# One exchange of maxima and sums for q's half rows, another order of the attention's slots, and the weights' sums one tile earlier

## The chip, the cores and the metric

The kernel runs on one core of a Trainium2 chip. The metric is the device time in microseconds (us) of one execution. The kernel before took 883.22 us (median of three runs, 882.94 to 884.86).

## What is computed

Eight batches go through a linear attention with eight heads, 576 rows and head dimension 64, and the 4608 rows that come out go through a feed-forward network with 512 model and 2048 inner columns:

```python
q_s = exp(q - max(q, axis=-1));  q_s = q_s / (sum(q_s, axis=-1) + 1e-09)
k_s = exp(k - max(k, axis=2));   k_s = k_s / (sum(k_s, axis=2) + 1e-09)
kv  = einsum('bhsd,bhse->bhde', k_s, v)
x   = einsum('bhsd,bhde->bhse', q_s, kv)      # rows of 512, one per token
h   = maximum(x @ w_in, 0.0)
out = h * h @ w_out
```

q is normalised along each row of 64 values, k along the 576 tokens. Everything is float32; a matmul is made of three passes over a high and a low part of its operands (wh·xh, wh·xl, wl·xh).

## The kernel before

**Tiles and chunks.** Seven tiles, t = 0 to 6, each take the first 512 tokens of batch t through the feed-forward network. A tile has 16 chunks f of 128 inner columns. In a chunk, TensorE (PE) makes `h` (`first`, line 994, 12 matmuls) and then the 12 matmuls of `second` (line 1016) that add an earlier chunk, f-2, to the four accumulators `acc`. At the beginning of a tile three `first` stand one behind another. ScalarE (ACT) makes `r` (Relu) and `gh` (Square), VectorE (DVE) makes `h` times `r` and `gl` (`split_g`, line 1009). `h` has two banks of PSUM, so `h` of chunk f needs `gl` of chunk f-2 to be done. `end_tile` (line 1328) finishes the last two chunks and stores the accumulators. Behind the seven tiles, the last full batch and a tile of all the remaining tokens are computed together with a Strassen-like scheme of seven products for each pair of chunks (lines 1494 to 1555); its operands (`b11`, `b21`, `t1` to `t4`, `b22`, each with a high and a low part) are prepared by `ahead` (line 1358) in the last chunks of tile 6 and by `late_part` (line 1409) behind it.

**Attention in slots.** Under the feed-forward work of tile t lies the attention of batch t+1, in 16 slots s, one per chunk; slot s belongs to head pair p = s // 4 and step i = s % 4. For batches from 2 on (`prepare`, `step`, `step_between`, `step_after`, lines 1227 to 1300):

- at i = 3 of the pair before: `k_max` on DVE, then `k_shift_pool` (line 737) on GpSimd (POOL): `partition_all_reduce` makes `kmx` from `km`, and k and the tail `kt` are shifted by it. `blocks_max` reduces q's half rows of 32 to their maxima and swaps them with the other half, by four DMAs of SyncE (SP).
- i = 0: `blocks_exp`: the larger maximum, subtraction, exp on ACT, sum, a second exchange of four DMAs.
- i = 1: `blocks_norm` and `blocks_turn` on DVE (transposed into `qT`), `k_exp` on ACT (`ek`), and the loads of the next pair's k and q.
- i = 2: for even p, `blocks_split`: `qh` on ACT and `ql` on POOL; the next pair's v is loaded (a small memset on POOL goes with it). For odd p, `kv_product` (line 880) of both pairs on PE, then `ks`, `kvh`, `kvl`.
- i = 3 of odd p: `x_product` of both pairs on PE.

**Weights' sums.** For the Strassen part, eight sets of sums of `w_in` are made in tiles 2 to 5, two sets a tile (`sums_step`, line 1337): `add_sums` on POOL (`full` and `sums`, six instructions) at f % 8 = 1, the rest at 2 to 4.

**Order.** Outside tile 0, where a planner sorts recorded work, each engine runs its instructions in the order in which the code tells them. Where a helper records a call, all instructions have line 100.

Of the kernel before, what the change touches and what calls it, by code (L numbers as in the profile page):

```python
# [336 lines left out]
def attention_ffn(  # L337
# [290 lines left out]
    def swap_halves(t, name):  # L628

        o = small([P, NG], "sw", f"sw_{name}", 1)  # L630
        for j in range(2):
            for a in range(2):
                at, of = j * D + a * Q, j * D + (1 - a) * Q
                Y.dma_start(out=o[at:at + Q], in_=t[of:of + Q])
        return o

    def blocks_max(b, p):
        mx = small([P, NG], "bmx", f"bmx_{b}_{p}", 1)
        V.tensor_reduce(out=mx, in_=made["q", b, p], op=ALU.max, axis=AX.X)
        made["bmx", b, p] = mx, swap_halves(mx, f"m_{b}_{p}")  # L640

    def blocks_exp(b, p):
        t = made["q", b, p]
        mx, sw = made.pop(("bmx", b, p))
        V.tensor_tensor(out=mx, in0=mx, in1=sw, op=ALU.max)
# [4 lines left out]
        sm = small([P, NG], "bsm", f"bsm_{b}_{p}", 1)  # L650
        V.tensor_reduce(out=sm, in_=t, op=ALU.add, axis=AX.X)
        made["bsm", b, p] = sm, swap_halves(sm, f"s_{b}_{p}")

    def blocks_norm(b, p):
        t = made["q", b, p]
        sm, sw = made.pop(("bsm", b, p))
        V.scalar_tensor_tensor(
            out=sm, in0=sm, scalar=EPS, in1=sw, op0=ALU.add, op1=ALU.add
        )
        V.reciprocal(out=sm, in_=sm)  # L660
        V.tensor_tensor(
            out=t, in0=t, in1=sm.unsqueeze(2).broadcast_to([P, NG, Q]), op=ALU.mult
        )
# [216 lines left out]
    def kv_product(b, p):  # L880
# [14 lines left out]
        with plan.together():  # L895
            for i, (k_part, v_part) in enumerate(parts):
                for j in range(2):
                    rows, cols = slice(j * D, (j + 1) * D), slice(j * D, j * D + n)
                    T.matmul(
                        out=ps[rows, cols], lhsT=k_part[:, rows],  # L900
                        rhs=vr[:, j, i, :] if b == 0 else v_part[:, cols],
                        start=(i == 0), stop=(b > 0 and i == C), n=2 * n,
                    )
            if b == 0:
                for j in range(2):
                    rows = slice(j * D, (j + 1) * D)
                    T.matmul(
                        out=ps[rows, rows], lhsT=ekt[:, rows],
                        rhs=v_heads[tl, 2 * p + j, 0:D].only(p // 2),
                        start=False, stop=True, n=2 * n,  # L910
                    )
        if b == 0:
            ks, at_of = made.pop(("ks", p)), D
        else:
            ks, at_of = small([P, 1], "ks", f"ks_{b}_{p}"), D + 1
            V.tensor_scalar_add(ks, ps[:, D:D + 1], EPS, n=8)
            V.reciprocal(out=ks, in_=ks, n=8)
# [12 lines left out]
        made["kv", b, p] = (kvh, kvl)  # L930

# [203 lines left out]
    def store(t, acc, c):  # L1135
        if c % 2 == 0:
            made["o"] = cvt.tile([P, 2, DM], F32, tag="w", name=f"o_{t}_{c}")
        o = made["o"][:, c % 2, :]
        if t == B and c == C - 1:
            V.tensor_copy(out=o[:, 0:DM // 2], in_=acc[c][:, 0:DM // 2])  # L1140
            S.copy(out=o[:, DM // 2:DM], in_=acc[c][:, DM // 2:DM])
        elif c % 2:
            S.copy(out=o, in_=acc[c])
        else:
            V.tensor_copy(out=o, in_=acc[c])
        if t < B:
            rows = out[t * SQ:t * SQ + M, :].rearrange(
                "(p c) e -> p c e" if t < TB else "(c p) e -> p c e", c=C
            )
            Y.dma_start(out=rows[:, c, :], in_=o)  # L1150
        else:
            per = P // TL
            for j in range(per):
                r0 = (c * per + j) * SQ + M
                queue = S if c == C - 1 and j % 2 else Y
                queue.dma_start(out=out[r0:r0 + TL, :], in_=o[j * TL:(j + 1) * TL, :])
# [40 lines left out]
    for p in range(NP):  # L1197
        plan.ease = p * STEP
        boot_max(p)
        boot_turn(p)  # L1200
        boot_exp(p)
        q_norm(0, p, G)
        kv_product(0, p)
        q_turn(0, p)
        x_product(0, p, x)
# [21 lines left out]
    def prepare(b, p):  # L1227
# [4 lines left out]
        if b >= TB:  # L1232
            blocks_max(b, p)
# [5 lines left out]
    def step(b, s):  # L1239

        p, i = divmod(s, NP)
        if b >= TB:
            if i == 0:
                blocks_exp(b, p)
# [18 lines left out]
    def step_after(b, s, x):  # L1263
# [16 lines left out]
        elif i == 2:  # L1280
            if b >= TB:
                if p % 2:
                    kv_product(b, p - 1)
                    kv_product(b, p)
            else:
                if p == 0:
                    tail_turn(b)
                kv_product(b, p)
# [7 lines left out]
        elif i == 3:  # L1296
            if b < TB or p % 2:
                x_product(b, p, x)
            if p + 1 < NP:
                prepare(b, p + 1)  # L1300
# [36 lines left out]
    def sums_step(t, f, begin=False):  # L1337

        j, i = divmod(f, NF // 2)
        j += 2 * (t - TB)  # L1340
        if t < TB or j >= NF // 2:
            return
        if begin:
            if i == 4:
                rest_sums(j)
            return
        if i == 1:
            add_sums(j)
        elif i == 2:
            begin_sums(j)  # L1350
        elif i == 3:
            split_sums(j)
        elif i == 4:
            keep_sums(j)

    x_of, w_of = {}, {}

    def ahead(f, x):

        k = range(2)  # L1360
        if f == 4:
            for i in range(2):
                to = slabs[X_RAW + i].bitcast(F32)[:, :, 0:(B - 1) * TL]
                Y.dma_start(out=to, in_=x_tail[:, 2 * i:2 * i + 2, 0:(B - 1) * TL])
            w_of[0] = weights(0)
            load_weights(0, w_of[0], "a11", "s1", "a12", "s2")
        elif f == 12:
# [5 lines left out]
            x_of["b11"] = pieces("b11", 0)  # L1373
            split_part(made["b11"], "b11", 0)
            split_part(made["b11"], "b11", 1)
        elif f == 13:
            made["sum"] = [att.tile([P, M], F32, tag=tag, name=f"sum_{tag}") for tag in ("k", "q")]
            for i in k:
                G.tensor_tensor(
                    out=made["sum"][i], in0=made["b12"][i], in1=made["b11"][i], op=ALU.subtract  # L1380
                )
        elif f == 14:
            x_of["t1"] = pieces("t1", 0)
            for i in k:
                split_part(made["sum"], "t1", i)
        elif f == 15:
            load_weights(0, w_of[0], "s3", "a22", "s4")
            for name in ("b21", "t2"):
                x_of[name] = pieces(name, 0)
            split_part(made["b21"], "b21", 0)  # L1390
            G.tensor_tensor(
                out=made["sum"][0], in0=made["b22"][0], in1=made["sum"][0], op=ALU.subtract
            )
            split_part(made["b21"], "b21", 1)
            V.tensor_tensor(
                out=made["sum"][1], in0=made["b22"][1], in1=made["sum"][1], op=ALU.subtract
            )
            for i in k:
                split_part(made["sum"], "t2", i)
            for i in k:  # L1400
                G.tensor_tensor(
                    out=made["b11"][i], in0=made["sum"][i], in1=made["b11"][i], op=ALU.subtract
                )
            for i in k:
                G.tensor_tensor(
                    out=made["b21"][i], in0=made["b21"][i], in1=made["sum"][i], op=ALU.subtract
                )

    def late_part(name, src):

        x_of[name] = pieces(name, 0)
        for i in range(2):
            split_part(made[src], name, i)

    for t in range(WT):
        b = t + 1
        x_next, acc = begin_next(t), begin_acc(t)
        parts = {}
        for f in range(NF):
            h = first(t, f, x)  # L1420
            sums_step(t, f, True)
            if f < LA:
                sums_step(t, f)
# [5 lines left out]
            step(b, f)  # L1429
            plan.due = None  # L1430
            if f >= LA:
                for c in range(C):
                    second(f - LA, parts[f - LA], acc, c)
                    if c == 0:
                        step_between(b, f, x_next)
                sums_step(t, f)
                parts[f] = split_g(t, f, *h)
            plan.due = f + SOON
            step_after(b, f, x_next)
            plan.due = None  # L1440
            if t == WT - 1:
                ahead(f, x_next)
        if t == 0:
            plan.run(SEEDS, fill)
            x = split_x(x_next, b)
        elif t < WT - 1:
            x = split_x(x_next, b)
        if t < WT - 1:
            if b + 1 < B:
                prepare(b + 1, 0)  # L1450
            end_tile(t, parts, acc, NF - 2, NF - 1)
    units = [(t, f, parts[f], acc, c, 0, NF - 1) for f in (NF - 2, NF - 1) for c in range(C)]
# [42 lines left out]
    for n in range(PAIRS):  # L1495
        one, two = 2 * n, 2 * n + 1
        w = w_of.pop(n)
# [6 lines left out]
        if n == 0:  # L1504
            unit(3)
# [3 lines left out]
        if n == 0:  # L1509
            late_part("t3", "b11")  # L1510
        unit(1)
# [6 lines left out]
        unit(1)  # L1518
        product(A, w["s2"], x_of["t2"], False)
        S.copy(out=u2, in_=A)  # L1520
        if n == 0:
            late_part("t4", "b21")
# [4 lines left out]
        unit(1)  # L1527
# [4 lines left out]
        if n == 0:  # L1532
            late_part("b22", "b22")
        else:
            unit(1)
# [77 lines left out]
```

## Time and profile before

| what | value |
|---|---|
| the profiled execution, device time | 882.38 us |
| its span, from the first to the last instruction | 880.2 us |
| median of the runs | 883.22 us |
| mean granted TensorE clock | 0.996 |
| idle DVE before the maxima's exchange, in all | 45.0 us in 18 waits |
| idle DVE before the sums' exchange, in all | 57.2 us in 23 waits |

The profile gives, for each engine, its busy time, and for each idle stretch the instruction or transfer that ended it. An engine that is busy nearly all the time sets the time of the kernel; what the other engines wait for matters only where that engine waits in turn. PE's clock is in the column PEclk, in shares of full speed. In the rows of a timeline the first number is the start in us, the second the duration, and a bracket holds the idle time before the row.

### The profile page before, as it was taken

To read this page: it belongs to the slowest core of one execution; us is meant where nothing else is said; L and a number is where in the kernel's file an instruction comes from. 1 tells how busy PE (TensorE), PEld (TensorE's weight loads), DVE (VectorE), ACT (ScalarE), POOL (GpSimd) and SP (SyncE) were. 2 spreads that over 40 slices of the span, in tenths; PEclk is the share of its full clock that TensorE was granted. 3 is DMA by queue.
4 is the path that set the end of the run, shared out by engine and by line. 5 is a ranking of instruction groups with operands and counts; after the bars stand their busy time and mean duration, and the time that the engine had idled before them with its cause. 6 is when DMAs were issued, how large, how long until landed. Compare 5 with 4: busy or idle time off the path is not lost.

```text
span 880.2 us, 12793 instructions
## 1 busy us (share of the span) xinstructions
PE 858.7 (98%) x4408; PEld 705.6 (80%) x4408; DVE 521.5 (59%) x936; ACT 368.0 (42%) x690; POOL 253.2 (29%) x300
## 2 busy tenths in 40 slices
PE   7899999999999999999999999999999989999997
PEld 7678888888887888788878888888888768888886
DVE  7998976555665566655665566556554783333421
ACT  5888854333434343434433343434333542222221
POOL 6789981111231304140414123130111321010000
PEclk9999999999999999999999999999999999999999
DMA  9991123211241244323331424124341057542432
GB/s 300 381 336 45 33 50 89 43 36 36 79 117 39 74 108 120 86 74 102 107 105 37 114 81 118 40 74 108 83 131 39 6 180 248 168 146 82 156 120 49
DMA packets 168977, 95.54 MB, mean 109 GB/s; under 512 B 117712, under 2 KB 150992, under 8 KB 168912
## 3 DMA queue, kind: packets, MB, share of 16 engines
q1 hardware_dynamic: 167200, 93.41, 36.6%
q10 hardware_dynamic: 1712, 1.31, 0.6%
q8 instruction: 35, 0.57, 0.3%
q14 instruction: 30, 0.25, 0.1%
HBM read 64.88 MB, written 29.23 MB: 107 GB/s over the span
## 4 chain that ended last, share of the span: by engine, by line
PE 72%; DVE 11%; DMA 5%; ACT 4%; SPq 4%; issue 4%; POOL 0%; DVEq 0%; ACTq 0%; POOLq 0%
PE acc L100 34%; PE h L100 24%; PE h L1129 8%; SPq L100 4%; PE x L100 2%; PE kv L100 2%; DMA sw_m<-bmx 2%; DMA sw_s<-bsm 1%; DVE km L100 1%; DVE bsm L100 1%; DVE gl L100 1%; DVE w L100 1%; DVE q L100 1%; DVE bmx L100 1%; ACT q L100 1%
## 5 line engine op out<-in xcount | busy, mean ns | idle before, releaser
L100 PE MATMUL acc<-w,gh 128*128 128x512 f32 x1152 | 355.8, 390 | 0.0
L100 PE MATMUL h<-xh,w 128*128 128x512 f32 x896 | 296.5, 393 | 3.9 <-DVE gl L100 3.8
L100 PEld LDWEIGHTS acc<-w,gh 128*128 128x128 f32 x1152 | 214.9, 188 | 43.8 <-ACT gh L100 0.4
L100 PE MATMUL acc<-w,gl 128*128 128x512 f32 x576 | 224.3, 389 | 0.0
L100 PEld LDWEIGHTS h<-xh,w 128*128 128x128 f32 x896 | 168.2, 188 | 42.7 <-DVE gl L100 7.3
L100 PE MATMUL h<-xl,w 128*128 128x512 f32 x448 | 174.6, 390 | 0.0
L100 PEld LDWEIGHTS acc<-w,gl 128*128 128x128 f32 x576 | 108.1, 188 | 23.1 <-DVE gl L100 0.4
L100 ACT ACTIVATE r<-h 128x512 f32<-128x512 f32 x112 | 66.1, 590 | 78.0 <-PE h L100 77.6
L100 DVE TENSOR_TENSOR gl<-h,gh 128x512 fp32r<-128x512 f32 x112 | 77.0, 688 | 36.4 <-ACT gh L100 29.6
L100 PEld LDWEIGHTS h<-xl,w 128*128 128x128 f32 x448 | 84.1, 188 | 16.2
L100 DVE SCALAR_TENSOR_TENSOR h<-h,r 128x512 f32<-128x512 f32 x112 | 77.0, 688 | 33.5 <-ACT r L100 32.7
L100 ACT ACTIVATE gh<-r 128x512 fp32r<-128x512 f32 x112 | 70.4, 629 | 52.9 <-PE acc L100 48.1
L100 POOL TENSOR_TENSOR k<-k,kmx 128x512 f32<-128x512 f32 x24 | 30.9, 1289 | 170.4 <-issue 120.6
L100 POOL PARTITION_ALL_REDUCE kmx<-km x24 | 17.5, 728 | 213.4 <-DVE km L100 143.4
L100 ACT ACTIVATE q<-q 128x576 f32<-128x576 f32 (+1 forms) x32 | 21.5, 672 | 98.4 <-DVE q L100 88.7
L100 DVE SCALAR_TENSOR_TENSOR bsm<-bsm,sw_s 128x18 f32<-128x18 f32 x24 | 11.0, 459 | 57.4 <-DMA sw_s<-bsm 57.2
L100 POOL TENSOR_TENSOR w<-w,raw 128x512 int32<-128x512 int32 x32 | 42.0, 1320 | 5.8 <-DVE w L100 2.8
L100 POOL TENSOR_TENSOR w<-w,w 128x512 fp32r<-128x512 f32 x32 | 41.1, 1299 | 6.2 <-ACT w L100 6.1
L1129 PE MATMUL h<-w,w 128*128 128x512 f32 x144 | 38.1, 401 | 2.5 <-DVE c L100 2.3
L100 POOL TENSOR_TENSOR gl<-c,gh 128x512 fp32r<-128x512 f32 x8 | 10.3, 1290 | 96.7 <-ACT gh L100 96.7
L100 ACT ACTIVATE raw<-raw 128x1024 f32<-128x1024 f32 (+1 forms) x32 | 36.2, 1147 | 0.6 <-DMA raw<-in_moe_w_in_dram 0.5
L100 DVE TENSOR_TENSOR c<-h,u_xh 128x512 f32<-128x512 f32 x16 | 11.1, 691 | 42.9 <-ACT u_xh L100 31.9
(152 smaller groups left out, 1003.6 us busy)
## 6 DMA issues: line engine op xcount, KB each, us to landing
k<-in_k_dram SPq DMA_DIRECT2D x32, 256.0 KB, 2.8
raw<-in_moe_w_in_dram SPq DMA_DIRECT2D x16, 512.0 KB, 8.6
raw<-in_moe_w_out_dram SPq DMA_DIRECT2D x16, 512.0 KB, 8.9
out_dram<-o SPq DMA_DIRECT2D x32, 256.0 KB, 2.5
v<-in_v_dram SPq DMA_DIRECT2D x56, 128.0 KB, 3.1
w<-w_sums SPq DMA_DIRECT2D x28, 256.0 KB, 3.5
q<-in_q_dram SPq DMA_DIRECT2D x96, 72.0 KB, 2.4
w_sums<-w SPq DMA_DIRECT2D x24, 256.0 KB, 2.7
```

Source lines behind the costliest of these rows:

```text
L100: getattr(self.eng, op)(*map(real, args), **{k: real(a) for k, a in kwargs.items()})
L1129: nc.tensor.matmul(out=out.real(), lhsT=a[:, k * P:(k + 1) * P].real(), rhs=m[k].real(), start=(begin and k == 0 and i == 0), stop=(k == 1 ...
```

## The change

**One exchange.** `blocks_exp` subtracts each half row's own maximum, without waiting for the other half, and takes exp. `blocks_swap` sums and then swaps maxima and sums together, in four DMAs. `blocks_norm` takes the larger maximum, rescales both sums by exp of the difference (a 36-column exp on ACT), and normalises.

**Order of the slots.** `blocks_exp` and, for p > 0, `blocks_swap` go into `prepare`. `step` of i = 0 and 1 stands behind `split_g`. The slots come from a list: in tiles 5 and 6 slots 3 and 11 of a batch share a chunk with slots 2 and 10. So batch 6 ends two chunks early in tile 5, batch 7 begins there, and ends at chunk 11 of tile 6. `prepare` of the next batch stands behind `end_tile`, and the copy of accumulator 0 goes from DVE to ACT in tiles 1 to 5. Where both pairs' `kv_product` stand together, both `ks` come ahead of both splits. In the Strassen part the operands are all split by chunk 15 but `t4`, and the units of leftover `second` work are dealt out anew for the first pair.

**Sums.** The weights' sums are made in tiles 1 to 4, `add_sums` at the end of chunks with f % 8 = 2, the others at 3, 4 and 7.

```diff
+    def blocks_exp(b, p):
+        t = made["q", b, p]
+        st = small([P, 5, NG], "bst", f"bst_{b}_{p}", 1)
+        mx = st[:, 0, :]
+        V.tensor_reduce(out=mx, in_=t, op=ALU.max, axis=AX.X)
...
+    def blocks_swap(b, p):
+        st = made["bst", b, p]
+        V.tensor_reduce(out=st[:, 1, :], in_=made["q", b, p], op=ALU.add, axis=AX.X)
...
+                Y.dma_start(out=st[at:at + Q, 2:4, :], in_=st[of:of + Q, 0:2, :])
...
     def blocks_norm(b, p):
...
+        V.tensor_tensor(out=by, in0=st[:, 0, :], in1=st[:, 2, :], op=ALU.max)
         V.tensor_tensor(
...
+            out=mx, in0=mx, in1=by.unsqueeze(1).broadcast_to([P, 2, NG]), op=ALU.subtract
+        )
+        S.activation(out=mx, in_=mx, func=AF.Exp)
+        V.tensor_tensor(out=sm, in0=sm, in1=mx, op=ALU.mult)
...
+        V.tensor_tensor(out=by, in0=by, in1=st[:, 0, :], op=ALU.mult)
...
+        for work in (kv_product, kv_scale, kv_split):
+            for p in pairs:
+                work(b, p)
...
-    def sums_step(t, f, begin=False):
+    def sums_step(t, f, end=False):
 
         j, i = divmod(f, NF // 2)
-        j += 2 * (t - TB)
-        if t < TB or j >= NF // 2:
+        j += 2 * (t - 1)
+        if t < 1 or j >= NF // 2:
             return
...
+        if end:
+            if i == 2:
+                add_sums(j)
...
+    for t in range(1, WT):
+        for f in range(NF):
+            turns[t, f] = []
+            while ORDER and (not turns[t, f] or (t >= WT - 2 and ORDER[0][1] in (3, 11))):
+                turns[t, f].append(ORDER.pop(0))
...
+            for b, s in todo[::-1]:
+                step_after(b, s, x_next, len(todo) == 1)
+                if s == NF - 1 and f < NF - 1 and b + 1 < B:
+                    prepare(b + 1, 0)
             plan.due = None
+            sums_step(t, f, True)
...
     for n in range(PAIRS):
         one, two = 2 * n, 2 * n + 1
+        units_at = (0, 1, 1, 1, 1) if n else (3, 0, 1, 0, 0)
```

On POOL in tile 4, around the all-reduce of batch 5's pair 1 (in a name the first number is the batch or the tile, the second the pair or the chunk). Before:

```order
L100 TENSOR_TENSOR sums_4_4434<-full_4_4431,sums_4_4434 128x256
L100 TENSOR_TENSOR ql_5_0_4476<-qT_5_0_4449,qh_5_0_4474 128x576
L100 MEMSET v_5_1_4501 128x4
L100 ISA
L100 ISA kmx_5_1_4543<-km_5_1_4540 128x128
L100 ISA
L100 TENSOR_TENSOR k_5_1_4451<-k_5_1_4451,kmx_5_1_4543 128x512
```

The same place in the change:

```order
L100 TENSOR_TENSOR ql_5_0_4465<-qT_5_0_4438,qh_5_0_4463 128x576
L100 MEMSET v_5_1_4487 128x4
L100 TENSOR_TENSOR full_6_4491<-w11_1343 128x512
L100 TENSOR_TENSOR full_6_4491<-w12_1421 128x512
L100 TENSOR_TENSOR sums_6_4494<-full_6_4491 128x256
L100 TENSOR_TENSOR sums_6_4494<-sums_6_4494,full_6_4491 128x256
L100 TENSOR_TENSOR sums_6_4494<-full_6_4491 128x256
L100 TENSOR_TENSOR sums_6_4494<-full_6_4491,sums_6_4494 128x256
L100 ISA
L100 ISA kmx_5_1_4537<-km_5_1_4534 128x128
L100 ISA
L100 TENSOR_TENSOR k_5_1_4440<-k_5_1_4440,kmx_5_1_4537 128x512
```

The six instructions of `add_sums` stood ahead of `ql` of pair 0; now they stand between it and the all-reduce of pair 1.

On PE in tile 6, the products kv of batch 7's pairs 0 and 1. Before:

```order
L100 MATMUL acc_6_3_6262<-w5_925,gl_6_4_6360 128x512
L100 MATMUL kv_7_0_6447<-v_7_0_6033,ek_7_0_6218 64x65 x8
L100 MATMUL kv_7_0_6447<-v_tail_115,kt_7_6037 64x65 x2
L100 MATMUL kv_7_1_6465<-v_7_1_6270,ek_7_1_6403 64x65 x8
L100 MATMUL kv_7_1_6465<-v_tail_115,kt_7_6037 64x65 x2
L100 MATMUL h_6_7_6487<-xh_6_0_6101,w6_1011 128x512
```

In the change:

```order
L100 MATMUL acc_6_3_6219<-w2_710,gl_6_1_6180 128x512
L100 MATMUL kv_7_0_6279<-v_7_0_5909,ek_7_0_6065 64x65 x8
L100 MATMUL kv_7_0_6279<-v_tail_115,kt_7_5913 64x65 x2
L100 MATMUL kv_7_1_6290<-v_7_1_6158,ek_7_1_6235 64x65 x8
L100 MATMUL kv_7_1_6290<-v_tail_115,kt_7_5913 64x65 x2
L100 MATMUL h_6_4_6319<-xh_6_0_6077,w3_797 128x512
```

They stood behind the accumulation of chunk 4 and ahead of h of chunk 7; now behind that of chunk 1 and ahead of h of chunk 4, three chunks earlier in the tile.

More of the change, by code (lines that the diff above doesn't have):

```diff
@@ L1202, in attention_ffn @@
         q_norm(0, p, G)
[L1203 removed]
+        kv_of(0, p)
         q_turn(0, p)
@@ L1372, in ahead @@
             )
-            x_of["b11"] = pieces("b11", 0)
-            split_part(made["b11"], "b11", 0)
-            split_part(made["b11"], "b11", 1)
-        elif f == 13:
[L1377 to L1381, printed above, removed]
+            for i in k:
+                to = slabs[X_RAW + i].bitcast(F32)[:, :, 0:(B - 1) * TL]
+                Y.dma_start(out=to, in_=x_tail[:, 2 * i:2 * i + 2, 0:(B - 1) * TL])
@@ new lines, in ahead @@
+            w_of[0] = weights(0)
+            load_weights(0, w_of[0], "a11", "s1", "a12", "s2")
+        elif f == 6:
+            split_x_of("b11")
+        elif f == 9:
+            temps = [att.tile([P, M], F32, tag=tag, name=f"sum_{tag}") for tag in ("k", "q")]
+            take("t1", G, temps, made["b12"], made["b11"])
+        elif f == 11:
+            split_x_of("t1")
+        elif f == 12:
+            split_x_of("b21")
+            take("t2", V, made["t1"], made["b22"], made["t1"])
+        elif f == 13:
+            split_x_of("t2")
+            take("t3", V, made["b11"], made["t2"], made["b11"])
@@ L1382, in ahead @@
         elif f == 14:
-            x_of["t1"] = pieces("t1", 0)
-            for i in k:
-                split_part(made["sum"], "t1", i)
+            split_x_of("t3")
+            take("t4", V, made["b21"], made["b21"], made["t2"])
         elif f == 15:
             load_weights(0, w_of[0], "s3", "a22", "s4")
[L1388 to L1413, printed above, removed]
+            split_x_of("b22")
+    ORDER = [(2, 0)]
+    for b in range(2, B):
+        ORDER += [(b, s) for s in range(NF)]
+    del ORDER[0]
+    turns = {}
+    for t in range(1, WT):
[3 more added lines that the diff above has]
+                turns[t, f].append(ORDER.pop(0))
@@ L1415, in attention_ffn @@
+    for f in range(NF):
+        turns[0, f] = [(1, f)]
     for t in range(WT):
-        b = t + 1
         x_next, acc = begin_next(t), begin_acc(t)
```

141 lines of the change are left out of this document (70 added, 71 removed).

## Prediction

> **What bounds the kernel now.** I read the page's first part, then PE's waits, then the timeline of one tile. The first row shows that PE is busy for 98% of the span; only PE's own idle time can be won.
>
> ```profile
> PE 858.7 (98%) x4408; PEld 705.6 (80%) x4408; DVE 521.5 (59%) x936; ACT 368.0 (42%) x690; POOL 253.2 (29%) x300
> ```
>
> PE's waits (in all, how often, longest) say what that idle time is:
>
> ```profile
> PE h L100 <- DVE gl L100: 3.8, 4, 2.1
> PE x L100 <- DVE kvl L100: 2.8, 4, 0.8
> PE h L1129 <- DVE c L100: 2.3, 1, 2.3
> ...
> PE x L100 <- ACT qh L100: 0.4, 1, 0.4
> ...
> PE x L100 <- DVE ql L100: 0.3, 1, 0.3
> ```
>
> The longest wait for `gl` lies in tile 0, which the change leaves as it is; another is in tile 3, where DVE stood before an exchange:
>
> ```profile
> 42.09 0.50 PE L100 MATMUL h<-xh,w 128*128 128x512 f32 x1 [2.06 <-DVE gl L100]
> ...
> 354.36 0.50 PE L100 MATMUL h<-xh,w 128*128 128x512 f32 x1 [1.10 <-DVE gl L100]
> ```
>
> The wait for `c` is where the Strassen part begins. In the windows behind it the seventh column, PEclk, is below 1:
>
> ```profile
> 712.00:714.00 2.00, 1.74 (x7) 1.13 (x7) 1.20 (x2) 1.31 (x3) 0.62 (x1) 0.87 0.00 0
> 714.00:720.00 6.00, 6.00 (x21) 4.84 (x22) 4.76 (x7) 3.87 (x8) 0.66 (x1) 0.76 0.63 200
> ```
>
> If the clock was either full or half, it was half for 2 × 2 × 0.13 + 2 × 6 × 0.24 = 3.4 us, and half of these, 1.7 us, is lost. So that gap of 2.3 us cost 4.0 us.
>
> **What the change wins.** Batch 7's attention ends four chunks sooner, so DVE prepares the Strassen operands in chunks 12 to 15 at some 1.4 to 2.8 us a chunk, and its work no longer piles up behind the last x: I take off the whole 4.0. The waits of x for `qh` and `ql` (0.4 + 0.3) are at the same place: 0.7. With both `ks` ahead of both splits, and no DMA wait ahead of them, `kvl` of pair 1 comes about 0.8 sooner: of the 2.8 us, 2.0 go. Of the waits for `gl`, 3.8 - 2.1 = 1.7 are behind tile 0, and I take 1.0, since DVE's work at i = 3 grows by a subtraction and a sum. Together 7.7 us; between 5 and 10.
>
> Against that, at the start of tile 6 DVE now has a whole `blocks_norm` ahead of the split of x, some 3.5 us where about 3 are free: +0.4 us (0 to 1.5). The exchange itself is off PE's path either way. SP issues four DMAs less for each pair, which frees it. `prepare` behind `end_tile` has DVE's 3 us under the 8.2 us of the three `first`: nothing, or +0.5 a tile, since the last of these needs `gl` of chunk 0. That bound goes into the range.
>
> **What it costs: the all-reduce.** POOL waits more than it works, but one chain through it is long. Tile 4 before, pair 1 of batch 5:
>
> ```profile
> 430.43 2.52 POOL L100 TENSOR_TENSOR full<-w 128x512 f32<-128x512 f32 x2
> ...
> 436.35 1.44 POOL L100 TENSOR_TENSOR ql<-qT,qh 128x576 fp32r<-128x576 f32 x1
> 437.74 0.10 POOL L100 MEMSET v<- 128x4 f32 x1
> 443.83 0.72 POOL L100 PARTITION_ALL_REDUCE kmx<-km  x1 [5.99 <-DVE sums L100]
> 451.69 1.28 POOL L100 TENSOR_TENSOR k<-k,kmx 128x512 f32<-128x512 f32 x1 [7.14 <-issue]
> ```
>
> The all-reduce starts 6.0 us after the memset ends, and the shift of k 7.86 us after the start of the all-reduce. In tile 1, without sums, it is the same:
>
> ```profile
> 151.50 0.10 POOL L100 MEMSET v<- 128x4 f32 x1
> 158.01 0.72 POOL L100 PARTITION_ALL_REDUCE kmx<-km  x1 [6.41 <-issue]
> ```
>
> So I read it as a preparation of 6 us that begins only when POOL's earlier instruction has ended, whatever the data does. The Trainium skill has such a price (GPSIMD Engine Reference, 2.1 Instruction dispatch): the first call after a code library is loaded pays about 6 us, 5.95 measured there, that no instruction shows. The gaps of 6.0 and 6.4 here agree, and here it comes back.
>
> The chain then goes to ACT and PE. These rows are, in order, the start of tile 4, its kv of pair 1, and `ek` of pair 1 on ACT:
>
> ```profile
> 421.00 0.39 PE L100 MATMUL h<-xh,w 128*128 128x512 f32 x1
> ...
> 454.42 0.64 PE L100 MATMUL kv<-v,ek 128*64 128x65 f32 x16
> ```
>
> ```profile
> 453.00 0.63 ACT L100 ACTIVATE ek<-k 128x512 f32<-128x512 f32 x1 [4.12 <-POOL k L100]
> ```
>
> `ek` ends at 453.63, PE wants it at 454.42: a slack of 0.8 us in a chain without any other. The change puts `add_sums` between `ql` of pair 0 and this all-reduce. It lasts 436.35 - 430.43 = 5.9 us. Part comes back, because `ql` comes sooner, for it no longer stands behind the sums and the exchange starts sooner:
>
> ```profile
> 425.38 0.69 DVE L100 TENSOR_TENSOR gl<-h,gh 128x512 fp32r<-128x512 f32 x1
> ...
> 427.71 0.75 DVE L100 TENSOR_REDUCE bsm<-q 128x18 f32<-128x576 f32 x1 [0.75 <-ACT q L100]
> ```
>
> ```profile
> L100 DVE TENSOR_TENSOR bmx<-bmx,sw_m 128x18 f32<-128x18 f32 x24 | 4.2, 176 | 45.0 <-DMA sw_m<-bmx 45.0
> ```
>
> The sum can follow `gl` at once, 1.6 us sooner. The exp now ahead of Relu takes 0.2 of that back, and four more small DVE operations at 0.18 and a small exp with its handoffs, estimated at 0.4, take 1.1. With some 0.5 that `ql` had waited for the sums, it is about 0.8 us sooner (0 to 1.5). PE then waits for 5.9 - 0.8 - 0.8 = 4.3 us, in each of tiles 1 to 4: 17.2 us. ACT stands in `ek` meanwhile; Relu of chunk 6 is behind it, but PE waits for kv anyhow.
>
> In tile 5 there are no sums, but slot 3 shares a chunk with slot 2, and kv comes one chunk earlier. A chunk is `h` and `acc`, from the chain of work that ended last:
>
> ```profile
> 238.46 2.72 PE acc L100 x12
> 241.18 2.72 PE h L100 x12
> ```
>
> That is 5.4 us: 5.4 - 0.8 - 0.8 = 3.8 us. In tile 6, kv comes three chunks earlier, 454.42 - 421.00 - 16.3 = 17.1 us from the tile's start. The rows of tile 6 before: its start, Relu and Square of chunk 0, and the group of `qh`:
>
> ```profile
> 611.73 0.39 PE L100 MATMUL h<-xh,w 128*128 128x512 f32 x1
> ```
>
> ```profile
> 614.65 0.60 ACT L100 ACTIVATE r<-h 128x512 f32<-128x512 f32 x1 [2.13 <-PE h L100]
> 615.28 0.63 ACT L100 ACTIVATE gh<-r 128x512 fp32r<-128x512 f32 x1
> ```
>
> ```profile
> L100 ACT CAST qh<-qT 128x576 fp32r<-128x576 f32 x24 | 16.2, 674 | 30.1 <-DVE qT L100 29.9
> ```
>
> `qh` follows Square, so it ends at 4.2 + 0.7 = 4.9 us, `ql` at 6.3, the all-reduce starts at 12.3, k at 20.2, and `ek` is done at 20.2 + 1.3 + 0.6 = 22.1: PE waits for 5.0 us.
>
> Pair 3 has more room. Its memset, its all-reduce, and its kv on PE in tile 4:
>
> ```profile
> 482.57 0.10 POOL L100 MEMSET v<- 128x4 f32 x1
> 490.35 0.79 POOL L100 PARTITION_ALL_REDUCE kmx<-km  x1 [7.67 <-issue]
> ```
>
> ```profile
> 502.76 0.64 PE L100 MATMUL kv<-v,ek 128*64 128x65 f32 x16
> ```
>
> With `ql` 1.0 us sooner and the sums behind it, POOL is free at 482.7 - 1.0 + 5.9 = 487.6, the all-reduce starts at 493.6 to 495.3 (6.0 or 7.7 us later), k 7.9 later and `ek` is done 2.0 after that: 503.5 to 505.2, against 502.8. I take 1.0 us in tiles 1 to 4 and 0.5 in tiles 5 and 6, where a chunk of 5.4 is lost and the sums of 5.9 are not there: 5.0 us together.
>
> **The clock behind the new gaps.** Six gaps of 3.8 to 5.0 us are longer than the 2.3 us behind which the clock fell, so each costs 1.7 us again: 10.2. The gap of 1.1 us in tile 3 shows no such loss, so pair 3's gaps get none. The Trainium skill (TensorE: Matmul & The Clock Gate, Part 1) says that the clock halves after at least one idle window of about 3.4 us, in a window that runs freely. By that rule a gap of 4.3 us would hold a whole window in about a quarter of the cases, and the loss would be some 2.6 us instead of 10.2. Here 2.3 us were enough, and the measurement decides.
>
> **The sum.** 17.2 + 3.8 + 5.0 + 5.0 + 10.2 = 41.2 us of new waits, less 7.7, plus 0.4: +33.9. The profiled execution took 882.38 us and would take 916.3; it lies 0.84 under the median of 883.22, so the forecast is 917.1.
>
> **Rivals.**
>
> *PE never waits for kv: faster.* If the preparation of the all-reduce can run while POOL still does the sums, or is not paid when POOL was busy just before, the all-reduce starts at about 437.8 - 0.8 + 5.9 = 442.9, `ek` ends at 452.8, ahead of 454.4, and tiles 5 and 6 come out in time as well. Only the gains are left: 883.2 - 7.7 + 0.4 = 875.9. It decides at a delay of 0.8 us. For it speaks that two tiles are a small sample of 24 all-reduces; against it, that both show 6 us or more with POOL idle and `km` long done. 0.12. If about half of each new wait of 2 to 3 us were left out together with the clock's loss, so that gains and losses meet, it would be about 883: 0.02.
>
> *The waits come, the clock holds.* Then it is 917.1 - 10.2 = 906.9, and with each of the six gaps 1 us shorter 901. Against it stands the drop behind 2.3 us. By the Trainium skill's rule on idle windows (TensorE: Matmul & The Clock Gate, Part 1) it would be 917.1 - 10.2 + 2.6 = 909.5. 0.18.
>
> *The waits are longer.* If the preparation takes 7.7 us as in pair 3's row, six gaps grow by up to 1.7 (10 us) and pair 3's reach 2.3, where the clock falls too (6 × 1.7 = 10): 917.1 + 20 = 937 at most. 0.16.
>
> The forecast itself, 907 to 927, has 0.52.
>
> **The numbers.** Faster or slower by over 0.2% is 1.8 us, about what a measurement of this kernel can tell from no change. Faster 0.12, same 0.02, slower 0.86. The range is 897 to 939: it takes in the case without the loss of clock and short gaps, and the longest gaps, and leaves out the two cases at or under 883.
>
> **What would show it.** Right: in PE's waits of the changed kernel, kv waiting for `ek` (or `kt`) some 25 us in six long waits, one in each of tiles 1 to 6 before kv of pair 1; POOL's all-reduce of pair 1 about 6 us after the last `sums`; windows with PEclk below 1 behind each gap; no wait of 2.3 us where the Strassen part begins. Wrong: an all-reduce that starts within a microsecond or two of the last `sums`, or `ek` of pair 1 done before kv's turn, with PE idle for less than 10 us behind tile 0. Longer waits of `h` for `gl` at the tiles' starts would say that DVE, not POOL, has become the bound.

## The result and the profile after

The changed kernel took 917.73 us (median of six runs, 915.1 to 920.24), the kernel before 883.05 us in the runs beside them (880.83 to 884.86): a ratio of 1.0397, with a 95% interval of 1.0374 to 1.0421. It is slower by 34.7 us. The profiled execution after took 920.24 us, with a span of 918.5 us and a mean granted clock of 0.981.

The first row of the page: PE's share of the span has fallen from 98% to 95%, and its busy time has risen by 17.6 us for the same 4408 matmuls.

```profile
PE 876.3 (95%) x4408; PEld 717.7 (78%) x4408; DVE 529.3 (58%) x1008; ACT 378.3 (41%) x719; POOL 244.1 (27%) x295
```

So time was lost in two ways, by waits and by slower matmuls. PE's waits (in all, how often, longest) name the first: kv, and nothing else of size. The waits for `c`, `qh` and `ql` are gone, and the one left for `gl` is that of tile 0. First the row of kv before, then the rows after:

```profile
PE kv L100 <- ACT ek L100: 0.5, 1, 0.5
```

```profile
PE kv L100 <- ACT ek L100: 17.3, 5, 4.4
PE kv L100 <- POOL v L100: 10.8, 4, 5.7
PE h L100 <- DVE gl L100: 2.0, 1, 2.0
...
PE x L100 <- DVE kvl L100: 0.7, 1, 0.7
```

Six of these waits are long, one in each of tiles 1 to 6, ahead of kv of pair 1: 4.43, 4.32, 4.33, 3.74, 3.34 and 5.69 us, 25.85 in all. "POOL v" in the second row is the memset that stands on POOL behind the shift of `kt`; in tiles 5 and 6 too `ek` ended just ahead of kv, so both rows mean one chain. POOL in tile 4, from `ql` of pair 0 to the shift of pair 1:

```profile
456.56 1.43 POOL L100 TENSOR_TENSOR ql<-qT,qh 128x576 fp32r<-128x576 f32 x1 [3.68 <-ACT qh L100]
457.93 0.10 POOL L100 MEMSET v<- 128x4 f32 x1
458.00 2.53 POOL L100 TENSOR_TENSOR full<-w 128x512 f32<-128x512 f32 x2
...
462.86 1.26 POOL L100 TENSOR_TENSOR sums<-full,sums 128x256 f32<-128x256 f32 x1
470.15 0.72 POOL L100 PARTITION_ALL_REDUCE kmx<-km  x1 [6.03 <-issue]
477.89 1.25 POOL L100 TENSOR_TENSOR k<-k,kmx 128x512 f32<-128x512 f32 x1 [7.03 <-issue]
```

`km` was done at 461.61, but the all-reduce starts 6.03 us behind the last `sums`, and k 7.74 us after that. ACT and PE follow at once:

```profile
479.18 0.63 ACT L100 ACTIVATE ek<-k 128x512 f32<-128x512 f32 x1 [7.41 <-POOL k L100]
```

```profile
479.86 0.69 PE L100 MATMUL kv<-v,ek 128*64 128x65 f32 x16 [3.74 <-ACT ek L100]
```

In the windows behind it the seventh column, PEclk, falls to about half. In the trace the clock is half in six stretches of 3.41 or 6.83 us, one that begins in or just behind each of these waits, 34.1 us in all, of which some 29.4 lie outside the waits.

```profile
480.00:482.00 2.00, 2.00 (x23) 1.68 (x22) 1.34 (x3) 1.12 (x3) 0.00 (x0) 0.62 0.45 136
482.00:484.00 2.00, 2.00 (x6) 1.52 (x5) 1.34 (x8) 1.23 (x4) 0.00 (x0) 0.53 0.88 142
```

The second kind of loss shows where the clock is full. In the last 28 us or so of each tile, and in parts of the Strassen part, 128x512 matmuls start some 233 ns apart and not 227. Over the whole trace that makes about 7 us, against about 1.5 before. I had not foreseen it.

### The profile page after: what moved, and what is told of

Its sections match the earlier page's. It is cut to its first block, busy times and chain, and to the rows that moved or that the text cites. A ratio compares the mean times of both kernels' runs of the same rounds, so it can differ in the third digit from the quotient of the medians.

```text
span 918.5 us, 12696 instructions
## 1 busy us (share of the span) xinstructions
PE 876.3 (95%) x4408; PEld 717.7 (78%) x4408; DVE 529.3 (58%) x1008; ACT 378.3 (41%) x719; POOL 244.1 (27%) x295
## 4 chain that ended last, share of the span: by engine, by line
PE 79%; issue 8%; DVE 6%; DMA 2%; POOL 2%; ACT 2%; SPq 1%; POOLq 0%; DVEq 0%; ACTq 0%
PE acc L100 36%; PE h L100 28%; PE h L1152 8%; PE x L100 3%; PE kv L100 2%; POOL k L100 1%; DVE bst L100 1%; SPq L100 1%; DVE h L100 1%; DVE km L100 1%; DMA raw<-in_moe_w_in_dram 1%; DMA bst<-bst 1%; DVE q L100 1%; DMA kt<-in_k_dram 1%; POOL kmx L100 1%
## 5 line engine op out<-in xcount | busy, mean ns | idle before, releaser
L100 PE MATMUL h<-xh,w 128*128 128x512 f32 x896 | 304.7, 403 | 2.0 <-DVE gl L100 2.0
L100 PEld LDWEIGHTS h<-xh,w 128*128 128x128 f32 x896 | 173.5, 194 | 41.2 <-DVE gl L100 2.5
L100 PE MATMUL h<-xl,w 128*128 128x512 f32 x448 | 179.3, 400 | 0.0
L100 PEld LDWEIGHTS h<-xl,w 128*128 128x128 f32 x448 | 87.0, 194 | 17.8
L100 PE MATMUL kv<-v,ek 128*64 128x65 f32 (+1 forms) x512 | 23.8, 241 | 28.1 <-ACT ek L100 17.3
L100 PEld LDWEIGHTS kv<-v,ek 128*64 128x64 f32 x512 | 19.5, 150 | 35.2 <-ACT ek L100 18.1
L100 DVE TENSOR_REDUCE bst<-q 128x18 f32<-128x576 f32 x48 | 35.9, 748 | 13.9 <-ACT q L100 13.5
L100 ACT ACTIVATE ek<-k 128x512 f32<-128x512 f32 x28 | 17.5, 623 | 62.1 <-POOL k L100 62.0
```

What stands on the lines that cost most here:

```text
L100: getattr(self.eng, op)(*map(real, args), **{k: real(a) for k, a in kwargs.items()})
```

## The experiments

**Taking the cause away: `ql` on VectorE.** `ql` of pairs 0 and 2 leaves POOL, so the sums can start as soon as POOL is free.

```diff
-        (V if p % 2 else G).tensor_tensor(out=ql, in0=qt, in1=qh, op=ALU.subtract)
+        V.tensor_tensor(out=ql, in0=qt, in1=qh, op=ALU.subtract)
```

> The changed kernel, with ql of the even pairs on DVE instead of POOL, so that on POOL nothing but a memset (and, in tiles 1 to 4, the sums) stands between the shift of pair 0's k and the all-reduce of pair 1. Theory A (the all-reduce needs some 6 us after POOL's earlier instruction, then 7.8 us to the shift, and that chain makes kv late): the sums now run from 10.4 to 16.4 us of the tile, the all-reduce starts at 22.4, ek of pair 1 is done at about 32, before PE wants it at 33.4; in tiles 5 and 6 the all-reduce starts 0.1 us after km and ek is done about 1 us early. All six long gaps (25.9 us) and their half clock (about 14 us) go: 876 us (873 to 880), and that is faster than the kernel before. Rival B (k is late for another reason: its load, ACT's queue, or the slots that share a chunk): the gaps stay at 20 us or more in all, 905 us or more. Rival C (DVE is the limit as soon as it has ql as well): the gaps for ek go, new waits of h for gl of 1 us and more a tile appear, 882 to 890.

It took 897.21 us, 1.0156 (1.0136 to 1.0176), outside all three ranges. All six long waits of kv are gone, as theory A has it. POOL in tile 4: the sums end at 451.02, and the all-reduce waits for nothing but `km` (the row's releaser), 0.14 us behind it.

```profile
445.46 2.52 POOL L100 TENSOR_TENSOR full<-w 128x512 f32<-128x512 f32 x2
...
450.28 0.74 POOL L100 TENSOR_TENSOR sums<-full,sums 128x256 f32<-128x256 f32 x1
457.40 0.73 POOL L100 PARTITION_ALL_REDUCE kmx<-km  x1 [6.38 <-DVE km L100]
```

But a new wait takes their place: h for `gl`, 2.95 to 3.48 us in each of tiles 1 to 4, with half clock behind three of them.

```profile
PE h L100 <- DVE gl L100: 14.6, 5, 3.5
```

Its main source are two small instructions of the new rescaling on DVE, of 18 and of 36 columns (a row of a timeline gives the form of the first alone). Beside POOL's `full`, the two of them take 3.38 us; for pair 1 of the same tile, with POOL idle, 0.40:

```profile
444.66 3.38 DVE L100 TENSOR_TENSOR bst<-bst 128x18 f32<-128x18 f32 x2 [1.70 <-DMA bst<-bst]
...
468.54 0.40 DVE L100 TENSOR_TENSOR bst<-bst 128x18 f32<-128x18 f32 x2
```

The first of them began while POOL shifted k and ended with that shift; the second took 2.94 us and ended with the second `full`. `gl` stands behind them on DVE. The Trainium skill (SBUF — State Buffer, section "SBUF: two separate sides") says that DVE instructions with two operands in SBUF and GpSimd share a pair of ports, an exclusive lock that the first holds for its whole instruction. The rows agree, with one thing more: the second had to let three POOL instructions pass (the shift of `kt` and both `full`). `ql`, now on DVE too, adds 0.76 us ahead of `gl`; it is not the main cause, since the next run has nearly the same waits with `ql` on POOL, and a later one (the earlier store) none of them with `ql` on DVE.

**Moving the sums back** from the end of the third chunk of each half tile to the end of the second (in `sums_step`, `i == 2` becomes `i == 1`).

> The changed kernel, with add_sums one chunk earlier (at the end of chunks with f % 8 = 1), so that on POOL it stands ahead of ql of pair 0 again; ql stays on POOL. Theory A: the four gaps of tiles 1 to 4 (4.4, 4.3, 4.3, 3.7) and their half clock (18.7 us at half, 9.3 lost) go, those of tiles 5 and 6 (3.3 and 5.7) stay: 917.7 - 16.8 - 9.3 = 891.6 us (888 to 895). Rival B (another reason than the place of the sums): nothing changes, 915 to 920.

909.07 us, 1.0302 (1.0273 to 1.033), between the two ranges. The waits of kv in tiles 1 to 4 go; those of tiles 5 and 6, which have no sums, stay (second row); and h waits for `gl` again, 2.57 to 2.94 us in tiles 1 to 4, where the pair of `bst` took 3.34 us in tile 3. So the order on POOL makes the waits of kv, and this place costs 11.0 us of waits in another way, in place of 16.8.

```profile
PE h L100 <- DVE gl L100: 13.8, 6, 2.9
PE kv L100 <- POOL v L100: 10.0, 4, 5.2
```

**Doubling the cause: a small POOL instruction ahead of each all-reduce**, on top of `ql` on VectorE. It copies one column of `km`; the all-reduce overwrites it.

```diff
+        G.tensor_copy(out=kmx[:, 0:1], in_=km[:, 0:1])
```

> As the kernel with ql on DVE, and with a copy of one column of km on POOL just ahead of each all-reduce, which needs km. Theory A: each all-reduce starts about 6 us behind this copy, not 0.1 us behind km: k of pair 1 is ready at 33.0 us of tiles 1 to 4 (gap 1.6), and the gaps of tiles 5 and 6 are 4.7 and 5.4 us; with the clock's loss 20 to 30 us more than without the copy, 896 to 906. Rival D (the preparation runs while POOL works or is not tied to its last instruction, and the sums were late by their own length alone): the copy costs its own 0.2 us, no gap, 876 to 878.

950.3 us, 1.0754 (1.0704 to 1.0804), beyond either figure and 53 us above the run without the copy. In every one of the 24 pairs the all-reduce starts 5.7 to 7.0 us behind the end of this copy. In tile 4, pair 0:

```profile
448.93 0.19 POOL L100 COPY kmx<-km 128x1 f32<-128x1 f32 x1 [14.83 <-DVE km L100]
456.06 0.72 POOL L100 PARTITION_ALL_REDUCE kmx<-km  x1 [6.94 <-issue]
```

A copy of 0.19 us costs 6 to 7 us, so it is not the length of POOL's earlier work that counts but when it ends. I had priced the waits of kv alone (26.5 us here). The late `ek` also holds up ACT, and with it `gl`: h waits 25.3 us, against 14.6 without the copy.

**The clock: filling the waits.** Transposes of the identity on PE ahead of kv of pair 1, into a bank that kv then overwrites, in tiles 1 to 6 (57, then 28 of them):

```diff
+        for _ in range(57 if b > 1 and p == 1 else 0):
+            T.transpose(out=ps[:, 0:P], in_=ident, identity=ident)
```

> The changed kernel, with 57 transposes of 128 columns added on PE ahead of kv of pair 1 in tiles 1 to 6; they write the bank that kv then overwrites, so they add work of about 3.2 us inside each gap and change nothing else. If the half clock behind the gaps comes of PE's idleness and costs about 14.7 us, the clock stays full behind the gaps that are shorter than 5 us, and 10 to 15 us are won although PE does more: 903 to 907 us. If the clock's fall has another cause, or its cost is small, the time stays within 915 to 920. If the gaps are not where I say, 57 transposes cost 6 x 3.2 = 19 us more: 937.

917.65 us, 1.0395 (1.0375 to 1.0415). By the time alone this would be the case in which the clock costs little. But the clock stays full (a mean of 1.000, against 0.981), and I had taken the price of a transpose wrongly: the 57 take 6.45 us, some 2 us longer than the wait, and give back what the clock gained:

```profile
170.73 6.45 PE L100 MATMUL kv<-ident 128*128 128x128 f32 x57
```

> The changed kernel with 28 transposes of the identity, instead of the 57 of e3_fill_gaps, put ahead of kv of pair 1 in tiles 1 to 6. In e3_fill_gaps the 57 took 6.45 us, 113 ns each and not the 57 ns that I had counted with, and so kept PE 2 us longer than the wait of 4.4 us; the clock stayed full all the same. Here they take 28 x 0.113 = 3.2 us, which leaves 1.1 us of each wait. Theory A (half clock costs half of the 29.4 us in which it lay outside the waits): full clock, waits of kv of 0.5 to 2.5 us, 917.7 - 14.7 = 903 us, 900 to 907. Rival B (the half clock costs nothing, since other waits take up what it loses): 917.7 within 0.4%. Rival C (transposes do not count as work for the clock when followed by a short wait): half clock stays and so do 917 us.

With 28 (3.28 us) it took 907.09 us, 1.0265 (1.0246 to 1.0283), just above the range of theory A. From tile 1 on the clock is full, and what is left of the waits has no half clock behind it:

```profile
174.30 3.28 PE L100 MATMUL kv<-ident 128*128 128x128 f32 x28
```

```profile
PE kv L100 <- ACT ek L100: 3.8, 4, 1.3
PE kv L100 <- POOL v L100: 3.4, 4, 1.3
```

Fillers (6 × 3.28 = 19.7) and waits ahead of kv of pair 1 (5.2) fill 25 us, as the waits alone did (25.85). So of the 10.6 us between the two kernels about 10 are the clock's.

**The wider spacing: where the weights start.** The new tile `bst` is 96 bytes longer than the three small ones that it replaces, as they are placed, and the slabs of weights for chunks 12 to 15 lie behind it. They start at address 195840 before, a multiple of 256, and at 195936 after, 32 beyond a multiple of 64. The padding tile ahead of them is made 8 floats shorter in the changed kernel (195904):

> The changed kernel with one padding tile 8 floats (32 bytes) smaller, nothing else. The four weight slabs of chunks 12 to 15 start at address 195936 in the changed kernel (32 beyond a multiple of 64; the new tile of maxima and sums is 96 bytes longer than the three it replaces take) and at 195840, a multiple of 64, in the kernel before; here they start at 195904, again a multiple of 64. In the changed kernel's trace the 128x512 matmuls of the last 28 us of each tile are spaced 232 ns apart and not 227, 7.1 us in all against 1.4 before. Theory A, the start of these slabs makes the spacing: 227 ns again everywhere, and 917.7 - 5.7 = 912 us. Rival B, the spacing comes of what other engines do in these stretches: it stays, and the time is 917.7 within 0.2%.

916.6 us, 1.0379 (1.0349 to 1.041), too close to the changed kernel to tell by time; the extra of the spacing is about 5 us in place of 7. Theory A is half right at this address. The clean test is the kernel before, with 8 floats more (195872):

```diff
-    tiny.pool.tile([P, 92], F32, tag="pad2", name="pad2")
+    tiny.pool.tile([P, 100], F32, tag="pad2", name="pad2")
```

> The kernel before with one padding tile 8 floats longer, nothing else: the weight slabs of chunks 12 to 15 then start at address 195872, 32 beyond a multiple of 64 as in the changed kernel, and no longer at 195840. In e5_align, with a start of 195904 (a multiple of 64 but not of 128), the extra time of the wider spaced 128x512 matmuls fell from 7.1 to 5.0 us, not to the 1.4 of before. Theory A (the start of the slabs makes the spacing): 232 ns in the last 28 us of each tile, about 7 us of extra in all and not 1.4, and 882.4 + 5.7 = 888 us. Rival B (something else in the changed kernel, such as its other order, makes most of it): spacing as before, 882.4 us within 0.2%.

887.17 us, 1.0045 (1.003 to 1.0059), so 4.0 us (2.6 to 5.2) for 32 bytes, as theory A expected. The spacing in the last 28 us of tile 3 goes from about 227.5 to 232.6 ns on average, and the extra to about 6 us in all. The padding moves every tile behind it; that the slabs are the ones that matter is read from where the wide spacing lies. The groups of `acc` matmuls in that stretch (the number behind the comma: mean ns of one), before and here:

```profile
L100 PE MATMUL acc<-w,gl 128*128 128x512 f32 x17 | 6.6, 390 | 0.0
```

```profile
L100 PE MATMUL acc<-w,gl 128*128 128x512 f32 x19 | 7.5, 395 | 0.0
```

**The parts by themselves, on the kernel before.** First the one exchange alone, with slabs at 195904, then the later place of the sums alone (`add_sums` from chunk 1 to the end of chunk 2 of each half tile).

> The kernel before with the one exchange alone (maxima and sums of the half rows swapped together, exp begun in the slot before, slots 0 and 1 done behind the second products), with the slabs of chunks 12 to 15 at a multiple of 64; the order of the slots, the sums and the Strassen part are as before. Theory A (my sum, the exchange's waits are all hidden and the gain of the change lies in the slots and the Strassen part): h's wait for gl gets 1.0 shorter and the halves of x's wait 0.7 go, 881 to 882.5 us, within 0.2% of before. Rival B (DVE and ACT do exp and sums a slot sooner, so the column maxima and the all-reduce behind them come later): kv waits in some tiles, 885 to 892 us.

891.99 us, 1.0109 (1.0085 to 1.0133): the end of theory B's range, but not its mechanism. kv does not wait; h waits for `gl` (11.4 us in place of 3.8), at the old place of the sums, where the pair of `bst` takes 3.12 us beside `full` in tile 4. The spacing adds some 3.5 us.

```profile
PE h L100 <- DVE gl L100: 11.4, 6, 2.6
```

> The kernel before with add_sums alone moved: from the end of chunk 1 of each half tile (behind its second products) to the end of chunk 2, the place that the change gives it, in tiles 2 to 5. Theory A (the all-reduce starts about 6 us behind POOL's previous instruction, and the sums are that instruction): the all-reduce of pair 1 starts some 5 to 6 us later and kv of pair 1 waits 4 to 5 us in four tiles, kv of pair 3 up to 3 us, with half clock behind the long ones; 905 to 935 us. Rival B (the all-reduce needs only the column maxima, 6 us is not held back by POOL's earlier work): 883 us within 0.3%.

917.77 us, 1.0393 (1.0361 to 1.0425): the number that I expected, but for another reason. No kv waits; h waits for `gl`, 14 times. In the kernel before, ACT splits the sums two chunks after POOL begins them, and this edit left that step where it was, so that ACT stood and waited for the sums, with `gh` behind it.

```profile
PE h L100 <- DVE gl L100: 30.4, 14, 3.1
```

```profile
251.88 1.14 ACT L100 CAST sums_h<-sums 128x512 fp32r<-128x512 f32 x2 [6.09 <-POOL sums L100]
```

So this run says nothing on kv. It shows only once more that the all-reduce follows the sums by 5.9 us (in tile 2 from 251.85 to 257.74).

**A place for the sums.** The changed kernel with `ql` on VectorE, and the even sums at the end of chunk 5 (in `sums_step` the even index counts from chunk 3, the odd from chunk 8, as before), the slabs at 195904.

```diff
+        for j, i in ((2 * t - 2, f - 3), (2 * t - 1, f - NF // 2)):
```

> The changed kernel with three repairs: ql of all pairs on VectorE; the sums of even index begun at the end of chunk 5, behind the memset that follows kv of pair 1, and no longer at the end of chunk 2 (those of odd index stay); the padding tile 8 floats smaller. Theory A (the loss is the sums in front of the all-reduce, the collision of the sums with the small VectorE instructions of the rescaling that run e1_ql_dve showed, and the spacing of 232 ns): no kv wait over 1 us, no h wait for gl over 1 us, clock full, 897.2 - 4 x 3.1 - 17/2 - 5.7 = 870.6 us, 867 to 875. Rival B (each place for the sums collides with something; behind kv it is the k shift of pair 2 or the rescaling of pair 1): one wait of 2 to 4 us per tile in four tiles with its clock loss, 885 to 897 us.

907.06 us, 1.0291 (1.0262 to 1.0319), above both ranges. On POOL the sums in fact stand behind the shift of pair 1 and ahead of the memset. Pair 1 is clear, but kv of pair 3 now waits 3.1 to 4.0 us in tiles 1 to 4. POOL in tile 4: the odd sums wait for a buffer that the store of the even sums still holds (the bracket), and the all-reduce of pair 3 follows them by 5.83 us.

```profile
508.53 2.58 POOL L100 TENSOR_TENSOR full<-w 128x512 f32<-128x512 f32 x2 [8.68 <-DMA w_sums<-sums_h]
...
513.41 1.26 POOL L100 TENSOR_TENSOR sums<-full,sums 128x256 f32<-128x256 f32 x1
520.50 0.72 POOL L100 PARTITION_ALL_REDUCE kmx<-km  x1 [5.83 <-issue]
```

So the store goes out two chunks sooner, and the padding tile is 24 floats shorter than in the changed kernel, which puts the slabs at 195840:

```diff
-            elif i == 7:
+            elif i == (7 if j % 2 else 5):
                 keep_sums(j)
```

> Run e8_ql_dve_sums_behind_kv with two edits: the stores of the even sums issued two chunks sooner (at chunk 8 and not 10), and the weight slabs of chunks 12 to 15 at 195840 as in the kernel before. In e8 the odd sums stood on POOL until the DMA of the even sums had let go of their buffer (8.68 us), ended 5.83 us ahead of the all-reduce of pair 3, and kv of pair 3 waited 3.82, 3.18, 4.04 and 3.07 us. Theory A (the same rule again: the all-reduce starts 6 us behind the end of POOL's earlier work): the odd sums end some 8 us sooner, all-reduces of pair 3 start 0.14 us behind the column maxima, the four waits and 17.1 us of half clock go, the spacing is 227 ns: 907.1 - 14.1 - 6 - 3.4 = 884 us, 877 to 889. Rival B (another wait takes the place): 895 us or more.

880.71 us, 0.9971 (0.9958 to 0.9984): within theory A's range, and faster than both kernels, than the one before by some 2.6 us. The all-reduces start 0.13 to 0.22 us behind `km`, but for the first, which starts 0.52 behind. No long wait of kv is left, the clock is full in all the tiles, and the spacing costs as little as before. What is left is x waiting for `kvh`, 3.2 us, and for `qh` and `ql`, 2.6: the pair of `bst` of pair 1 now stands beside the sums.

```profile
445.99 0.73 POOL L100 PARTITION_ALL_REDUCE kmx<-km  x1 [8.59 <-DVE km L100]
```

```profile
455.36 2.71 DVE L100 TENSOR_TENSOR bst<-bst 128x18 f32<-128x18 f32 x2
```

Last, the exchange alone again, with this place for the sums and the slabs at 195840:

> Run e6_exchange_alone (the kernel before with the one exchange) with two edits: the even sums put behind the k shift of pair 1 (end of chunk 5) and the odd ones at chunk 10, as in e11_keep_sooner, and the weight slabs of chunks 12 to 15 at 195840. In e6 the sums stood at chunk 1, beside the seven small VectorE instructions of the rescaling of pair 0, and h waited for gl 1.71, 2.50, 2.56 and 1.86 us in four tiles, with 6.8 us of half clock, and the wider spacing took 5.0 us against 1.4. Theory A (the exchange costs time only where its small VectorE instructions stand beside POOL's sums): these waits, the half clock and the spacing go, and 892.0 - 8.6 - 3.4 - 3.6 = 876, to which come up to 5 us of waits of x for kvh as in e11: 876 to 884 us. Rival B (the exchange costs by its added instructions, wherever the sums stand): 888 to 892 us.

896.77 us, 1.0137 (1.01 to 1.0175): both theories miss. The waits for `gl` of tiles 2 to 5 are gone and the spacing is as before, but x waits for `kvl`, about 1 us at a time, and the clock falls behind some of these.

```profile
PE x L100 <- DVE kvl L100: 12.6, 13, 1.1
```

The two small instructions take 0.40 us in all the tiles with sums, but this place is not wholly clear of the exchange either: in tile 4 the multiplication of q by the scale, which takes 0.76 us in the other tiles with sums, met `full`.

```profile
457.57 3.46 DVE L100 TENSOR_TENSOR q<-q,bst 128x576 f32<-128x576 f32 x1
```

What the exchange costs where no sums stand beside it thus stays open. In the order of before, neither place that I tried was free of a wait.

## Why the prediction was right

The forecast was 917.1 us, the result 917.73. The steps, in us:

| step | forecast | measured |
|---|---|---|
| kv of pair 1, tiles 1 to 4 | 17.2 | 4.43 + 4.32 + 4.33 + 3.74 = 16.8 |
| tile 5 | 3.8 | 3.3 |
| tile 6 | 5.0 | 5.7 |
| kv of pair 3 | 5.0 | 0.49 + 1.29 = 1.8, in tiles 5 and 6 alone |
| clock | 10.2 | about 10 by the fillers; 29.4 / 2 = 14.7 by the clock of the profiled run |
| start of tile 6 | 0.4 | no wait |
| gains | -7.7 | waits 3.8 + 2.8 + 2.3 + 0.4 + 0.3 less 2.0 and 0.7, and 1.7 of clock: -8.6 |
| wider spacing | not in the sum | 4.0 by times, some 5.5 by the trace |

For the profiled run, the trace's own figures give 25.85 + 1.8 + 14.7 + 5.5 - 8.6 = 39.3 against 918.5 - 880.2 = 38.3 us of span. For the medians, with the clock and the spacing as the runs' times give them, it is 25.85 + 1.8 + 10 + 4.0 - 8.6 = 33.1 against 34.7. What the clock costs, 10 or 14.7, the runs do not settle: four of the other five runs show the mean clock of the profiled one, 0.981.

*The preparation of the all-reduce* was read rightly: about 6 us that begins only when POOL's earlier instruction has ended. The rival that it could run beside the sums is refuted by POOL's rows after, and by the run with the small copy. The runs with `ql` on VectorE and with the earlier store show the other side: where POOL has been free for some 6 us, the all-reduce starts with the data. The Trainium skill (GPSIMD Engine Reference, 2.1 Instruction dispatch) gives such a price for the first call after a code library is loaded; in these traces each all-reduce that came close behind other POOL work paid it, 5.8 to 6.3 us behind the last `sums` or `ql` in the changed kernel.

*Tile 6* was built up in the prediction from single rows. POOL's rows after, with the tile's start at 643.55, give `ql` done 6.3 us into the tile and the all-reduce started at 12.5, as forecast; only k came later, 8.42 us after the start of the all-reduce and not 7.86, so the wait was 5.69 and not 5.0.

```profile
648.42 1.43 POOL L100 TENSOR_TENSOR ql<-qT,qh 128x576 fp32r<-128x576 f32 x1 [10.04 <-ACT qh L100]
656.07 0.72 POOL L100 PARTITION_ALL_REDUCE kmx<-km  x1 [6.22 <-issue]
664.49 1.25 POOL L100 TENSOR_TENSOR k<-k,kmx 128x512 f32<-128x512 f32 x1 [7.70 <-issue]
```

*Pair 3* was put too high: in tiles 1 to 4 its kv did not wait at all. In tile 4 its all-reduce came 5.8 us behind the sums, as said, and `ek` ended 0.5 us ahead of kv:

```profile
512.02 0.74 POOL L100 TENSOR_TENSOR sums<-full,sums 128x256 f32<-128x256 f32 x1
518.56 0.88 POOL L100 PARTITION_ALL_REDUCE kmx<-km  x1 [5.80 <-DVE sums L100]
```

```profile
527.55 0.63 ACT L100 ACTIVATE ek<-k 128x512 f32<-128x512 f32 x1 [3.26 <-POOL k L100]
```

```profile
528.65 0.64 PE L100 MATMUL kv<-v,ek 128*64 128x65 f32 x16
```

I had worked with the old timetable. After the wait at pair 1 everything comes later in the tile (which starts at 442.55): POOL is free 70.2 us into it and not 66.6, and PE reaches kv of pair 3 at 86.1 and not 81.8. That leaves 15.9 us for the chain from POOL to `ek`, where I had 15.2, and the chain took 15.4, where I had 15.9 to 17.6: the 7.7 us of a single row of before did not come back.

*The clock.* The row of before decided rightly against the sparser rule of the Trainium skill (TensorE: Matmul & The Clock Gate, Part 1): all six gaps of 3.3 to 5.7 us were followed by half clock. The size, 1.7 us for each, agrees with the fillers' 10 us for six. By the rows of the clock it is low: four of the six stretches lasted 6.83 us and not 3.41, which makes 14.7. The rival in which the clock holds is refuted.

*What failed without showing in the total*: I did not look at where the tiles lie in memory. The missing 4 us of the spacing and the 3.2 us too many for pair 3 nearly cancel, so the closeness of the total is partly luck. And that the exchange is off PE's path either way holds for this order of the work, in which only the wait for `gl` of tile 0 is left, but not in general: by itself, in the order of before, it made h wait 11.4 us for `gl` and not 3.8.

## What to carry over

Where an instruction pays for a start that begins only when its engine is free, the end of the work ahead of it counts and not the length: keep such an engine free for that time ahead of it, or move the work behind it, and then look for what stands beside the new place. Small instructions on one engine can stand for the whole of a long one on another, so a moved block has to be checked against its neighbours on other engines and not on its own alone. When a change replaces small tiles by another, see where the large ones behind them have come to lie.

## What was not expected of the hardware

- The start of a slab of weights: matmuls of 128x512 that read slabs from addresses 32 beyond a multiple of 64 start some 233 ns apart, from a multiple of 256 227.5. At 195904, a multiple of 64 but not of 128, the extra was in between (about 5 us, against 7 and 1.5). Four places were tried, and why they differ the runs do not show.
- Two DVE instructions of 18 and 36 columns in SBUF take 3.4 to 4.1 us beside the shift and both `full` on POOL (pair 0 in tiles 1 to 4 of the run with `ql` on VectorE), and 0.40 us with POOL idle.
- The clock was half for 3.41 or 6.83 us at a time (once 10.24, in the run with the small copy), one, two or three of the windows of some 3.4 us that the Trainium skill names (TensorE: Matmul & The Clock Gate, Part 1). But no window had to be idle as a whole: in e12_exchange_sums_moved, waits of 0.62 and 1.09 us, 1.7 us apart, were enough in tile 4, though two of 1.10 us, as far apart, were not in tile 2, nor were waits of 1.2 to 1.3 us by themselves in the run with 28 transposes.
